# The order and the place of sixteen weight-band loads at the start of a fused spectral mixing and feed-forward kernel

## The chip, the cores and the metric

The kernel runs on one core of one Trainium2 chip. The metric is the device time of one execution in microseconds (us). Work is split over TensorE (PE; its weight loads are listed apart as PEld), VectorE (DVE), ScalarE (ACT), GpSimd (POOL) and SyncE (SP), whose queue issues every DMA of this kernel.

## The reference

For x of 8 batches x 3008 positions x 256 channels:

```python
X = np.fft.rfft(x, axis=1)
Yr = Xr @ w_r - Xi @ w_i + b_r
Yi = Xr @ w_i + Xi @ w_r + b_i
Y  = soft_threshold(Yr, 0.01) + 1j * soft_threshold(Yi, 0.01)
y  = np.fft.irfft(Y, n=3008, axis=1)            # 24064 tokens x 256
h  = y @ w_in                                   # 256 -> 2048
out = (h * np.clip(h + 3, 0, 6) / 6) @ w_out    # 2048 -> 256
```

All is float32, except that `w_in` and `w_out` arrive as float64.

## The kernel before

The 3008 positions are treated as 47 x 64. Stage 1 (`stage1`, seven sets for a batch, each loaded as a tile `xin`, or `x_hi`/`x_lo` for batch 0) does the transforms of length 47 and stores to a scratch tensor. `middle` (twelve pairs of frequency groups for a batch) loads a pair (`bt`, `f`), transforms over 64 (tile `X`), multiplies with the 256 x 256 weights (tiles `ps_a`, `tc`), applies the threshold, brings the parts into place (`zt`, by small DMAs, or for batch 0's last two pairs by VectorE copies on L482), transforms back (PE L498) and stores `pt` to a second scratch tensor. `segment` (seven for a batch) loads from there (`qt`, L531, two loads each) and does the inverse transform of length 47 into `raw` tiles of 512 tokens, on VectorE L562 and L574. `prepare` makes from a `raw` tile the seven operands `yb` of a Strassen-Winograd product. Then the feed-forward runs in units: 47 token chunks of 512 times 8 slices f of the hidden width. Unit (c, f) multiplies with `w_in` slice f (`phase_a` to `phase_d`, PE L165, sums on DVE L621), goes through the gate (ACT L680, DVE L682, ACT L136, DVE L137) and three units later is multiplied with `w_out` slice f (`down`, PE L711).

Every float32 operand is split in a high and a low half (`split`: high by an ACT copy, low by a DVE or POOL subtraction on L137), and a product is three matmuls.

The weights arrive as 16 bands of 512 KB in float64, eight of `w_in` and eight of `w_out`, band f of each for slice f; they are written below as in0 to in7 and out0 to out7. `decode` loads a band (`st`, L208) and turns the doubles into floats: per band two DVE operations on the words (L220, L221), three ACT operations, two DVE operations (L225, L229) and one on POOL (L230); an in-band then has four POOL subtractions (L247) and three splits, an out-band one split. `turn` moves each band in work one step on and, if told to, starts the next one from the list `bands`; its argument names the buffers that the band borrows: `EARLY` is `raw` for the load and three `yb`, `LATE` takes three sets of buffers by turns. The bands are started between the pairs of batch 0 and after that between the phases of the first units. A load of a band is put behind one chosen DMA on SP's queue (`tc.issue_after`).

The order on each engine's queue is made by a scheduler at build time from the program order, priorities, the buffers that are free and its own estimate of times; a queue then runs in that order. So loads may leave much earlier than the program text suggests, when their buffer is free, and an instruction that waits holds up all behind it on its queue.

In the kernel before the bands come in the order in0, in1, out0, in2, out1, in3, out2, in4, out3, in5, out4, in6, out5, in7, out6, out7. Two are started before batch 0's pairs, five between the pairs, three right after `prepare(0)`, the rest in the first units. Batch 1's stage 1 runs its first four sets among batch 0's pairs, the fifth `xin` is loaded after them with nothing that holds it back.

Of the kernel before, what the change touches and what calls it, by code (L numbers as in the profile page):

```python
# [101 lines left out]
def spectral_ffn(ctx: ExitStack, tc: tile.TileContext, x, w_r, w_i, bias, w_in, w_out, f47, f64, g64, sgn, out):  # L102
    nc = tc.nc
# [11 lines left out]
    def space(shape, dt, name, tag=None):  # L115
        tag = tag or name
        return sb.tile(shape, dt, name=name, tag=tag, bufs=depth.get(tag, 1))

    def twin(shape, dt, name, tag=None):

        t = space([P, 2, *shape[1:]], dt, name, tag)
        return t[:, 0], t[:, 1]

    def room(wide=False):
        if wide:
            return ps_b.tile([P, 512], F32, name="pb")
        return ps_a.tile([P, 512], F32, name="ps_a")

    def idle(q):

        pool, name = ((ps_o, "po0"), (ps_o, "po1"), (ps_c, "pd"), (ps_c, "pc"))[q % 4]
        return pool.tile([P, 512], F32, name=name)

    def split(hi, lo, src, on=None):

        nc.scalar.copy(out=hi, in_=src)  # L136
        (on or nc.vector).tensor_tensor(out=lo, in0=src, in1=hi.bitcast(F32), op=ALU.subtract)  # L137
# [38 lines left out]
    def run(g):  # L176
        for _ in g:
            pass

    nf = NFT // 2  # L180
# [22 lines left out]
    def decode(src, cut, tags):  # L203


        st = space([P, 2, 256, 2], I32, "st", tags[0])
        with tc.issue_after(stores[soon[made[0]]].ins if made[0] < len(soon) else pairs[1].ins):
            nc.sync.dma_start(out=st.rearrange("p a c w -> p a (c w)"), in_=cut(src, 2))  # L208
        yield
        high = st[:, :, :, 1]  # L210
        e = space([P, 2, 256], I32, "e", tags[1])
        m, r = (
            twin([P, 2, 256], I32, "m", tags[2])
            if len(tags) == 3
            else [space([P, 2, 256], I32, n, t) for n, t in zip("mr", tags[2:])]
        )
        mf, rf = m.bitcast(F32), r.bitcast(F32)
        v, s = nc.vector, nc.scalar

        v.tensor_scalar(out=e, in0=high, scalar1=20, scalar2=0x7FF, op0=ALU.arith_shift_right, op1=ALU.bitwise_and)  # L220
        v.tensor_scalar(out=m, in0=high, scalar1=0xFFFFF, scalar2=0xFFFFF, op0=ALU.bitwise_and, op1=ALU.bitwise_and)  # L221
        yield
        s.activation(out=rf, in_=e, func=AF.Relu, bias=top[:, :1], scale=-1.0)
        s.activation(out=e, in_=rf, func=AF.Relu, bias=top[:, 1:], scale=-(2.0**23))
        v.scalar_tensor_tensor(out=e, in0=high, scalar=-(1 << 31), in1=e, op0=ALU.bitwise_and, op1=ALU.bitwise_or)  # L225
        halves = st.rearrange("p a c w -> p (a c w)").bitcast(U16).rearrange("p (a c w) -> p a c w", a=2, w=4)
        s.activation(out=rf, in_=halves[:, :, :, 1], func=AF.Copy, bias=1.0, scale=2.0**-36)
        yield
        v.scalar_tensor_tensor(out=mf, in0=m, scalar=2.0**-20, in1=rf, op0=ALU.mult, op1=ALU.add)  # L229
        nc.gpsimd.tensor_tensor(out=mf, in0=mf, in1=e.bitcast(F32), op=ALU.mult)  # L230
        return mf, e.bitcast(F32)
# [22 lines left out]
    def out_band(f, tags):  # L254
        def cut(t, words):
            n = 512 * words
            return t[:, f * n : (f + 1) * n].rearrange("p (h c) -> p h c", h=2)

        w, _ = yield from decode(w_out, cut, tags)
        yield  # L260
        split(*(cut(t, 1) for t in wout_s), w)

    EARLY = (("raw", "yb", "yb", "yb"),)
    LATE = (("X", "bt", "tc"), ("z", "bt", "zt", "pt"), ("xin", "e", "xs"))
    bands = [(in_band, 0), (in_band, 1)]
    for f in range(nf):
        bands.append((out_band, f))
        if f + 2 < nf:
            bands.append((in_band, f + 2))
    bands = iter(bands)  # L270

    made, busy, ready, pairs, soon = [0], [], set(), [], (3, 8)

    def turn(how=None):

        for job in list(busy):
            if next(job[0], busy) is busy:
                busy.remove(job)
                ready.add(job[1])
        if how and made[0] < 2 * nf:  # L280
            make, f = next(bands)
            g = make(f, how[made[0] % len(how)])
            next(g)
            busy.append((g, (make, f)))
            made[0] += 1
# [6 lines left out]
    scr1, scr2, stores = {}, {}, []  # L292
# [7 lines left out]
    def stage1(b):  # L300
        scr1[b] = dram.tile([2, N1, NK, D], F32, name="scr1")
        sets = SEGS[-1:] + SEGS[:-1]
        xins = {}

        def load(i):
            n1, n = sets[i]
            rows, w = (R47, 2 * D) if n == 2 * J else (n * NK, D)
            if b == 0:
                xins[i] = spare[i]
            else:  # L310
                xins[i] = space([P, 2, 2 * D], F32, "xin", "raw" if b == 1 and i < 4 else "xin")
            at = n1 // J * 2 * D
            src = x[b, :rows, at : at + 2 * w].rearrange("p (s c) -> p s c", s=2)
            nc.sync.dma_start(out=xins[i][:rows, :, :w], in_=src)
            return rows, w

        shapes = [load(i) for i in range((len(sets), 2, 1)[min(b, 2)])]
        for i, (n1, n) in enumerate(sets):
            rows, w = shapes[i]
            xin = xins.pop(i)  # L320
            plus, minus = xin[:rows, 0, :w], xin[:rows, 1, :w]
            whole = b == 0 or b == 1 and i < 4
            e = space([P, 2 * D], F32, "e", "r" if whole else "e")[:rows, :w]
            on = nc.vector if whole else nc.gpsimd
            on.tensor_tensor(out=e, in0=plus, in1=minus, op=ALU.add)  # L325
            on.tensor_tensor(out=plus, in0=plus, in1=minus, op=ALU.subtract)
            for c, src in enumerate((e, plus)):
                q = 2 * i + c
                if whole:
                    ps = idle(q) if b else room(c == 1)  # L330
                    turns = f47_s[2][:rows, c * R47 : c * R47 + rows]
                    nc.tensor.matmul(out=ps[:rows, :w], lhsT=turns, rhs=src, start=True, stop=True)
                else:
                    xs = [t[:rows, :w] for t in twin([P, 2 * D], F32R, "xs")]
                    split(*xs, src, nc.gpsimd)
                    yield
                    ps = room()
                    product(ps[:rows, :w], [([t[:rows, c * R47 : c * R47 + rows] for t in f47_s[:2]], xs)], whole=True)
                home = ("a", "h", "z", "h", "xs", "h", "X")[q % 7] if b == 0 else "yb" if whole else "a"
                a = space([P, 2 * D], F32, "a", home)[:rows, :w]  # L340
                if home == "X":
                    space([P, 48], F32, "gap")
                nc.scalar.copy(out=a, in_=ps[:rows, :w])
                dst = scr1[b][c, n1 : n1 + n].rearrange("(g j) k d -> (j k) g d", g=w // D)
                stores.append(nc.sync.dma_start(out=dst, in_=a.rearrange("p (g d) -> p g d", d=D)))
                if c and i + 1 < len(sets) and i + 1 >= len(shapes) and not whole:
                    shapes.append(load(i + 1))
                yield
            if whole and len(shapes) < min(len(sets), 5 if i == 3 else i + 3 if i < 2 else 0):
                shapes.append(load(len(shapes)))  # L350

    bias_s = const.tile([P, 2 * D], F32, name="bias")
    sgn_s = const.tile([P, NK], F32, name="sgn")
# [33 lines left out]
    for n in range(2 * len(soon)):  # L387
        turn(EARLY if n < len(soon) else None)
    g64_s = g64_t[:2]
# [132 lines left out]
    def segment(b, k, tag="qt", aside=None):  # L522
        n1, n = SEGS[k]
        gr = 2 if n == 2 * J else 1
        rows = n // gr * NK
        w = n * NK
        t0 = b * S + n1 * N2
        qt = space([P, 2, 2, D], F32, "qt", tag)
        for cs in range(2):
            src = scr2[b][cs, n1 : n1 + n].rearrange("(g j) k d -> (j k) g d", g=gr)  # L530
            nc.sync.dma_start(out=qt[:rows, cs, :gr], in_=src)  # L531
        for c in range(t0 // T, (t0 + n * N2 - 1) // T + 1):
            if c not in raw:
                raw[c] = space([P, 2, T], F32, "raw")
# [11 lines left out]
        for dh in range(2):  # L546
# [3 lines left out]
                    out=ps[:, cs * w + g * rows : cs * w + (g + 1) * rows],  # L550
# [15 lines left out]
            for c, q, lo, hi in places(w, n * m):  # L566
                while lo < hi:
# [3 lines left out]
                    else:  # L571
# [3 lines left out]
                        out=raw[c][:, dh, q : q + size].rearrange("p (n q) -> p n q", n=r1 - row),  # L575
# [13 lines left out]
    yb = {}  # L589
# [157 lines left out]
    for i in range(3 * (NK // 2)):  # L747
        next(mid)
        if i % 3 == 0:
            turn(LATE[2:] if i == 27 else EARLY if i == 3 or i % 9 == 0 else None)  # L750
    run(mid)
    rest = stage1(1)
    for _ in range(8):
        next(rest)
# [146 lines left out]
```

## Time and profile before

| | us |
|---|---|
| median of 3 runs | 2559.48 (2558.84 to 2559.91) |
| profiled execution, its own time | 2560.95 |
| span of its trace | 2559.2 |
| PE busy in the span | 2502.8 (98%) |
| DVE busy | 1965.0 (77%) |
| ACT busy | 1825.9 (71%) |
| POOL busy | 756.2 (30%) |

Engines, lines and tiles are named as in the trace: "PE L498 pb<-zt" is a matmul on line 498 that reads `zt` and writes `pb`. A bracket at the end of a row tells how long the engine was idle ahead of it, and what it waited for. Names on the trace leave the band's number out: `st<-in_w_in` is the load of some band of `w_in`. SPq is SyncE's queue of DMA issues.

### The profile page before, as it was taken

What the parts mean: (1) busy time and instruction counts of PE and PEld (TensorE: products, weight loads), DVE (VectorE), ACT (ScalarE), POOL (GpSimd) and SP (SyncE); (2) the same over time, 40 slices, a digit from 0 to 9 for tenths busy, and PEclk for the clock granted to TensorE, in tenths of its full rate; (3) what the DMA queues carried; (4) which work ended last, traced back from release to release, by engine and by line L of the source; (5) the groups of instructions that cost most, each with busy time, mean ns of one, the idle gap of its engine ahead of it and who ended that gap; (6) DMA issues with size and microseconds to landing.
All of it is one profiled execution on the core that took longest, in us unless ns stands there. A gap on an engine that the chain in (4) does not pass through costs nothing.

```text
span 2559.2 us, 53456 instructions
## 1 busy us (share of the span) xinstructions
PE 2502.8 (98%) x20910; PEld 2447.6 (96%) x20910; DVE 1965.0 (77%) x3191; ACT 1825.9 (71%) x3587; POOL 756.2 (30%) x738
## 2 busy tenths in 40 slices
PE   6789999999999999999999999999999999999999
PEld 4579999999999999999999999999999999999999
DVE  7778878877787777777787777777777778677766
ACT  5467777777777777777777777777777777777776
POOL 3253342333223332323323333223321221121310
PEclk8889999999999999999999999999999999999999
DMA  7733432332222222333222222222222121110000
GB/s 244 224 88 103 126 103 83 91 91 68 60 84 78 86 72 67 85 86 89 60 75 84 72 79 84 71 78 80 74 78 59 53 66 51 37 41 17 12 18 17
DMA packets 150259, 200.54 MB, mean 78 GB/s; under 512 B 16863, under 2 KB 104215, under 8 KB 150007
## 3 DMA queue, kind: packets, MB, share of 16 engines
q1 hardware_dynamic: 150007, 197.13, 26.7%
q8 instruction: 164, 2.69, 0.5%
q14 instruction: 88, 0.72, 0.1%
HBM read 97.45 MB, written 74.97 MB: 67 GB/s over the span
## 4 chain that ended last, share of the span: by engine, by line
PE 90%; DMA 3%; DVE 3%; ACT 1%; POOL 1%; issue 1%; SPq 1%; ACTq 0%; POOLq 0%; DVEq 0%
PE po L711 38%; PE pb L165 19%; PE pc L165 10%; PE ps_a L145 7%; PE ps_a L165 7%; PE pd L165 5%; PE ps_a L142 3%; DMA xin<-in_x 1%; DMA zt<-tc 1%; DMA qt<-scr 0%; DMA x_lo<-in_x 0%; DVE r L682 0%; ACT r L680 0%; POOL e L325 0%; ACT gs L136 0%
## 5 line engine op out<-in xcount | busy, mean ns | idle before, releaser
L711 PE MATMUL po<-gs,w_out_hi 128*128 128x256 f32 x5984 | 1025.6, 277 | 0.0
L711 PEld LDWEIGHTS po<-gs,w_out_hi 128*128 128x128 f32 x5984 | 839.2, 188 | 1.6
L682 DVE SCALAR_TENSOR_TENSOR r<-r,h 128x1024 f32<-128x1024 f32 x375 | 476.4, 1270 | 269.4 <-ACT r L680 267.4
L711 PE MATMUL po<-gs,w_out_lo 128*128 128x256 f32 x2992 | 594.8, 278 | 0.9 <-ACT gs L136 0.5
L680 ACT ACTIVATE r<-h,three 128x1024 f32<-128x1024 f32 x375 | 433.0, 1155 | 191.5 <-DVE h L621 189.4
L165 PE MATMUL pb<-yb,w_in_hi 128*128 128x256 f32 x3008 | 568.2, 278 | 0.0
L137 DVE TENSOR_TENSOR gs<-r,gs 128x1024 fp32r<-128x1024 f32 x375 | 483.5, 1289 | 90.9 <-ACT gs L136 87.1
L136 ACT CAST gs<-r 128x1024 fp32r<-128x1024 f32 x375 | 394.3, 1051 | 109.3 <-DVE r L682 106.6
L165 PEld LDWEIGHTS pb<-yb,w_in_hi 128*128 128x128 f32 x3008 | 458.1, 189 | 3.1
L711 PEld LDWEIGHTS po<-gs,w_out_lo 128*128 128x128 f32 x2992 | 456.0, 188 | 3.8 <-ACT gs L136 2.2
L165 PE MATMUL pb<-yb,w_in_lo 128*128 128x256 f32 x1504 | 426.3, 286 | 2.0 <-ACT u L616 1.3
L137 POOL TENSOR_TENSOR yb<-T,yb 128x256 fp32r<-128x256 f32 x184 | 168.3, 917 | 841.9 <-ACT yb L136 828.2
L621 DVE TENSOR_TENSOR h<-pc,u 128x256 f32<-128x256 f32 x752 | 314.2, 418 | 113.1 <-PE pc L165 106.8
L616 ACT COPY u<-pb 128x256 f32<-128x256 f32 x752 | 279.5, 373 | 94.4 <-PE pb L165 80.5
L165 PE MATMUL pc<-yb,w_in_hi 128*128 128x256 f32 x1504 | 295.7, 278 | 0.0
L165 PEld LDWEIGHTS pb<-yb,w_in_lo 128*128 128x128 f32 x1504 | 283.5, 189 | 8.7 <-ACT u L616 2.8
L165 PEld LDWEIGHTS pc<-yb,w_in_hi 128*128 128x128 f32 x1504 | 228.9, 189 | 0.7
L165 PE MATMUL pc<-yb,w_in_lo 128*128 128x256 f32 x752 | 214.6, 285 | 4.7 <-DVE h L621 4.6
L616 ACT COPY p<-pb 128x256 f32<-128x256 f32 x376 | 140.1, 373 | 77.0 <-PE pb L165 75.1
L654 ACT COPY h<-pb 128x256 f32<-128x256 f32 x376 | 141.3, 376 | 49.4 <-PE pb L165 47.6
L621 DVE TENSOR_TENSOR h<-pd,p 128x256 f32<-128x256 f32 x376 | 156.6, 417 | 13.9 <-ACT p L616 11.8
L165 PEld LDWEIGHTS pc<-yb,w_in_lo 128*128 128x128 f32 x752 | 141.9, 189 | 9.4 <-DVE h L621 8.1
(165 smaller groups left out, 3939.4 us busy)
## 6 DMA issues: line engine op xcount, KB each, us to landing
bt<-scr SPq DMA_DIRECT2D x96, 256.0 KB, 3.0
scr<-pt SPq DMA_DIRECT2D x96, 256.0 KB, 2.4
zt<-tc SPq DMA_DIRECT2D x376, 64.0 KB, 2.0
out<-ot SPq DMA_DIRECT2D x93, 256.0 KB, 2.3
scr<-a SPq DMA_DIRECT2D x96, 240.0 KB, 2.7
qt<-scr SPq DMA_DIRECT2D x96, 240.0 KB, 3.5
xin<-in_x SPq DMA_DIRECT2D x42, 480.0 KB, 4.4
f<-in_f SPq DMA_DIRECT2D x96, 128.0 KB, 2.8
```

Of the source, the lines that this page charges most:

```text
L136: nc.scalar.copy(out=hi, in_=src)
L137: (on or nc.vector).tensor_tensor(out=lo, in0=src, in1=hi.bitcast(F32), op=ALU.subtract)
L142: first = first()
L145: m()
L165: last = nc.tensor.matmul(**m)
L616: nc.scalar.copy(out=t, in_=ps)
L621: nc.vector.tensor_tensor(out=to, in0=ps, in1=keep.pop((i, n)), op=ALU.add)
L654: marks["h", i] = nc.scalar.copy(out=hs[i][:, 1, :H], in_=pb)
L680: nc.scalar.activation(out=r, in_=h, func=AF.Relu, bias=three, scale=1.0)
L682: nc.vector.scalar_tensor_tensor(out=r, in0=r, scalar=6.0, in1=h, op0=ALU.min, op1=ALU.mult)
L711: last = nc.tensor.matmul(out=pos[dh][half], lhsT=w[:, ft * D + dh * P : ft * D + (dh + 1) * P], rhs=g[:, low, u, cols], start=opens and n ...
```

## The change

Four edits. The bands are sorted by `due`: in-band f at f, out-band f at f + 2.5, which gives in0, in1, in2, out0, in3, out1, in4, out2, in5, out3, in6, out4, in7, out5, out6, out7. Nine bands instead of seven are started by the end of batch 0's pairs: the two ahead of them, then steps 0, 3, 9 and 18 with `EARLY` buffers, 24 and 30 with `z` for the load and three `yb`, 27 with `xin`, `e` and `xs`; and `while busy: turn()` writes out what is left of them ahead of batch 1's first stage-1 sets and of the segments. A band started once the first two segments have been written is put behind the last of their four loads (`loads[3]`) instead of behind the second pair load. And the extra `xin` load of stage 1 (batch 1's fifth set) is put behind the last segment load written so far.

```diff
         st = space([P, 2, 256, 2], I32, "st", tags[0])
-        with tc.issue_after(stores[soon[made[0]]].ins if made[0] < len(soon) else pairs[1].ins):
+        if made[0] < len(soon):
+            ahead = stores[soon[made[0]]]
+        else:
+            ahead = loads[3] if loads else pairs[1]
+        with tc.issue_after(ahead.ins):
             nc.sync.dma_start(out=st.rearrange("p a c w -> p a (c w)"), in_=cut(src, 2))
...
+    def due(band):
+
+        make, f = band
+        return (f, 0) if make is in_band else (f + 2.5, 1)
+
     EARLY = (("raw", "yb", "yb", "yb"),)
     LATE = (("X", "bt", "tc"), ("z", "bt", "zt", "pt"), ("xin", "e", "xs"))
-    bands = [(in_band, 0), (in_band, 1)]
-    for f in range(nf):
-        bands.append((out_band, f))
-        if f + 2 < nf:
-            bands.append((in_band, f + 2))
-    bands = iter(bands)
-
+    SPARE = {i: ((("z", "yb", "yb", "yb"),), LATE[2:])[i // 3 % 2] for i in (24, 27, 30)}
+    bands = iter(sorted([(in_band, f) for f in range(nf)] + [(out_band, f) for f in range(nf)], key=due))
+
+    loads = []
...
             if whole and len(shapes) < min(len(sets), 5 if i == 3 else i + 3 if i < 2 else 0):
-                shapes.append(load(len(shapes)))
+                with tc.issue_after(loads[-1].ins) if loads else nullcontext():
+                    shapes.append(load(len(shapes)))
...
-            nc.sync.dma_start(out=qt[:rows, cs, :gr], in_=src)
+            loads.append(nc.sync.dma_start(out=qt[:rows, cs, :gr], in_=src))
...
         if i % 3 == 0:
-            turn(LATE[2:] if i == 27 else EARLY if i == 3 or i % 9 == 0 else None)
+            turn(SPARE[i] if i in SPARE else EARLY if i == 3 or i % 9 == 0 else None)
     run(mid)
+    while busy:
+        turn()
     rest = stage1(1)
```

## Rows read from the trace of the kernel before

**Rows 1.** The page: TensorE's busy tenths in 40 slices of 64 us.

```profile
PE   6789999999999999999999999999999999999999
```

**Rows 2.** Stages: busy of PE, PEld, DVE, ACT, POOL; clock, DMA share, GB/s.

```profile
64.00:76.00 12.00, 8.74 (x60) 7.14 (x58) 9.23 (x17) 5.12 (x12) 4.01 (x5) 0.94 0.84 234
112.00:126.00 14.00, 3.44 (x6) 0.83 (x4) 13.03 (x22) 9.85 (x20) 7.32 (x8) 0.63 0.84 260
134.00:165.00 31.00, 23.94 (x119) 20.26 (x118) 30.48 (x56) 22.68 (x50) 21.49 (x18) 0.72 0.29 82
165.00:204.00 39.00, 37.82 (x304) 36.10 (x305) 25.64 (x38) 28.19 (x56) 15.95 (x17) 1.00 0.29 78
```

**Rows 3.** TensorE's waits from 134 to 180 us: total, times, longest.

```profile
PE pc L165 <- DVE h L621: 4.6, 5, 1.7
PE pd L165 <- DVE h L621: 1.4, 1, 1.4
```

**Rows 4.** TensorE in order of time: start, duration, what, wait.

```profile
77.09 2.04 PE L498 MATMUL pb<-zt,g_all 128*128 128x512 f32 x2 [3.63 <-DMA zt<-tc]
...
112.38 1.02 PE L498 MATMUL pb<-zt,g_all 128*128 128x512 f32 x2
116.20 2.05 PE L498 MATMUL pb<-zt,g_all 128*128 128x512 f32 x2 [2.81 <-DVE zt L482]
126.09 0.78 PE L142 MATMUL ps_a<-f_all,qt 120*128 120x120 f32 x2 [7.84 <-DMA qt<-scr]
```

**Rows 5.** SyncE's queue in order of time: start, time to issue, what.

```profile
65.17 0.60 SPq L208 DMA_DIRECT2D st<-in_w_in  x1
...
118.90 0.32 SPq L501 DMA_DIRECT2D scr<-pt  x1
120.07 0.36 SPq L314 DMA_DIRECT2D xin<-in_x  x1
121.74 2.82 SPq L531 DMA_DIRECT2D qt<-scr  x4
124.66 0.38 SPq L208 DMA_DIRECT2D st<-in_w_out  x1
```

**Rows 6.** Landing us (last): load of 65.17, first qt, qt of 129.89.

```profile
st<-in_w_in SPq DMA_DIRECT2D x1, 512.0 KB, 9.3
...
qt<-scr SPq DMA_DIRECT2D x1, 240.0 KB, 4.3
...
qt<-scr SPq DMA_DIRECT2D x2, 240.0 KB, 3.2
```

**Rows 7.** VectorE in order of time, and one row of ScalarE.

```profile
111.99 0.42 DVE L221 TENSOR_SCALAR m<-st 128x512 int32<-128x512 int32 x1
...
115.47 0.59 DVE L482 COPY zt<-tc 64x256 f32<-64x256 f32 x2
...
129.47 0.36 ACT L560 COPY odd<-ps_a 128x240 f32<-128x240 f32 x1 [0.98 <-PE ps_a L145]
...
130.42 1.48 DVE L220 TENSOR_SCALAR e<-st 128x512 int32<-128x512 int32 x1 [1.58 <-DMA st<-in_w_out]
...
134.05 0.42 DVE L221 TENSOR_SCALAR m<-st 128x512 int32<-128x512 int32 x1
...
164.87 1.42 DVE L137 TENSOR_TENSOR w_out_lo<-m,w_out_hi 128x512 fp32r<-128x512 f32 x1
```

**Rows 8.** Decoding operations: ns min/median/max, first and last start in us.

```profile
L221 DVE TENSOR_SCALAR m<-st x7: 412/419/609, 112.0 to 152.1; 128x512 int32<-128x512 int32 x7
L225 DVE SCALAR_TENSOR_TENSOR e<-st,e x7: 676/942/1358, 116.1 to 156.6; 128x512 int32<-128x512 int32 x7
...
L137 DVE TENSOR_TENSOR w_in_lo<-m,w_in_hi x16: 285/540/1501, 28.2 to 154.0; 128x256 fp32r<-128x256 f32 x8, 128x128 fp32r<-128x128 f32 x8
L137 DVE TENSOR_TENSOR w_in_lo<-e,w_in_hi x8: 675/684/1771, 30.3 to 162.8; 128x512 fp32r<-128x512 f32 x8
...
L137 DVE TENSOR_TENSOR w_out_lo<-m,w_out_hi x8: 673/950/1750, 46.1 to 164.9; 128x512 fp32r<-128x512 f32 x8
```

## The prediction

> **What bounds the kernel now.** I read the page's tenths first. TensorE is at 90% or more in every slice but the first three [rows 1], so whatever this change does must show in the first 190 us or so: there TensorE stands still or runs slowly, and behind it a gain or loss only shifts the rest. Next the stages [rows 2]. From 112 to 126 TensorE is busy 3.4 of 14 us: this is the passage from batch 0's last pair to its first segment. From 134 to 165, the first units, it is busy 23.9 of 31 us at a mean granted clock of 0.72, so part of the time at the lower of its two levels, 1.2 instead of 2.4 GHz. From 165 it is busy 37.8 of 39 us at 1.00. In both troubled stretches VectorE is the full one: 13.0 of 14 and 30.5 of 31 us. From 165 to 204 it has 13.4 us free.
>
> Then the waits in order of time [rows 4]. The last pair's matmuls wait 2.81 us for a VectorE copy of `zt`; the first segment's wait 7.84 us for a `qt` load. Later, in the units, TensorE waits for the sums on VectorE, 6.0 us in six waits [rows 3]. There is one such place among the pairs too: 3.63 us at 77 us, for a `zt` transfer [rows 4].
>
> What VectorE does in that time is read from its own order [rows 7] and the decoding rows [rows 8]. L221 runs seven times from 112 us on: seven of the sixteen bands are decoded after 112, nine before. The bands' load order on SyncE's queue [rows 5] puts one `xin` load 1.7 us ahead of the four segment loads.
>
> **The change, part by part.** Nine bands also go with batch 0's pairs afterwards; seven stay, out3, in6, out4, in7, out5, out6, out7, and these may be loaded only behind the segment loads at about 122. So the edit moves no decoding out of the start as a whole. It clears it out of 112 to 126 and puts it behind. I go along the path.
>
> *Last pair.* Between 111.99 and the end of the last `zt` copy at 116.06 VectorE runs five word operations of bands, L220 and L221 [rows 7, 8]; one begins 0.33 to 0.45 us after the other, together 1.8 us. None can be there when no band's load is let through before the segments: -1.8. Bounds 0 (other work takes the places) and -2.8 (all of TensorE's wait [rows 4]).
>
> *Last matmuls.* Those at 112.38 took 1.02 us for two, those at 116.20, after 2.81 us of idling, 2.05: twice as long, the lower clock level [rows 4]. With a wait of 1.0 us instead of 2.8 I take the upper level: -1.0. Bounds 0 and -1.0.
>
> *Segment loads.* The first `qt` load, issued behind the `xin` load, took 4.3 us; two that were issued when little else moved took 3.2 [rows 5, 6]. The `xin` load now goes behind: -1.1. Bounds 0 and -2.0.
>
> *First segment's sums.* ScalarE's copy `odd` was done at 129.83, but VectorE's next instruction was L220 of a band whose load had been issued after the `qt` loads; it waited 1.58 us and took 1.48, so the segment's sums began 2.0 us late [rows 5, 7]. The same can come back, with another band in that place. I take it as gone: -2.0, with bounds -2.0 and +4.0. The upper one: three loads of 512 KB follow each other behind the segment loads, at 260 GB/s [rows 2] 2.0 us apart; now the first of such loads is waited for, and if it were the third, the sums would begin 4.0 us later still.
>
> *Pairs.* At 65.17 the tenth band's load is issued; it needed 9.3 us to land, in a stretch where the DMA engines are 84% busy [rows 2, 5, 6], and TensorE's wait of 3.63 us for `zt` ends it. A tenth band is now not loaded before the segments. Its 512 KB at 234 GB/s are 2.2 us of queue: -2.2. Against this, the nine hold six in-bands instead of five. By the undisturbed times an in-band costs VectorE 0.42 x 2 + 0.68 x 2 + 0.54 x 2 + 0.68 = 4.0 us, an out-band 0.42 x 2 + 0.68 x 2 + 0.67 = 2.9 [rows 8], with L220 and L229 taken as L221 and L225: +1.1. Together -1.1; bounds -3.6 (the whole wait) and +4.0 (one in-band's decoding stands fully in the pairs' way).
>
> The five gains make -7.0.
>
> *The seven bands in the first units.* Two in-bands and five out-bands cost 22.5 us by the undisturbed times. They will not be undisturbed: from 134.05 to 164.87 the trace holds 20 decoding instructions (the first and the last in [rows 7]), 17.8 us long where the undisturbed times give 11.7, a factor of 1.52. GpSimd is busy 21.5 of 31 us there [rows 2]. So 34 us against 17.8 there before: 16 us more. About 5 us of it fits between the first landing of a band and the first unit. Of the other 11, two thirds find room after 165, where VectorE has 13.4 us free [rows 2]: with three sets of buffers the seven go in three rounds, and only the first two need be over by then. Of the last third, 3.7 us, TensorE feels what it felt before: 6.0 us of waits for 17.8 us of decoding [rows 3, 7], 0.34 for each: +1.3. Bounds 0 (all hidden) and +5.4 (16 x 0.34). If the cover is gone, that is what it costs.
>
> The Trainium skill speaks against this part (SBUF — State Buffer, section "Who interferes with whom"): a VectorE instruction with two inputs in SBUF and a GpSimd instruction that reads SBUF share a read port, and whichever comes second stands still until the first is done. The trace agrees in kind: the same split on L137 took 673 to 1750 ns [rows 8]. By that rule the whole of GpSimd's 21.5 us could fall on the decoding, 44 us instead of 34, and the sum would be 1.1 us worse (10 / 3 x 0.34).
>
> The sorting itself costs nothing in issue: the same sixteen loads. No band is late by it: out3 and in6, loaded at about 124, are wanted by unit 6, and six units need 126 matmuls of `phase_a` to `phase_d` alone (seven products of three each), more than the 119 of all kinds that the stage to 165 holds [rows 2]. The extra `xin` load, now behind bands, feeds batch 1, whose next stage starts many units on; behind it on GpSimd stand its own sums.
>
> Sum: -7.0 + 1.3 = -5.7. The profiled execution took 2560.95, which gives 2555.3; it stands 1.5 above the median, so the median goes from 2559.48 to **2553.8**, 0.22% down. A change under 0.2%, 5.1 us, can hardly be told from none for this kernel.
>
> **Rivals.**
> *Gain kept whole* (0.09): the bands hide fully and the pairs gain all of their wait: -7.0 - 2.5 = -9.5, 2550. For it: VectorE's 13.4 us. Against: a queue in fixed order takes decoding when it is ready.
> *VectorE gives it back* (0.20): the 16 us fall where VectorE is full, +5.4: -1.6, 2557.9. For it: 30.5 of 31 us busy [rows 2]. Against: the seven are wanted later than that.
> *The way is not cleared* (0.09): the last pair and the segments wait for something else as long, the loads land as late, and only the pairs' -1.1 stays: 2558.4.
> *Bands ahead of the first gates* (0.18, slower): out3, in6 and out4 are written right after `prepare(0)`, ahead of unit 0, so they may stand on VectorE's queue before the first units' gates. Their 9.8 us times 1.52 are 14.9 us in which nothing reaches the second multiplication: -7.0 + 14.9 = +7.9, 2567. It decides from 12 us of decoding ahead of the first gate. For it: the program order, and that all three are loaded together. Against: bands stood in that place before too, and TensorE's longest wait for a sum was 1.7 us [rows 3].
>
> **How the numbers follow.** The forecast has 0.44, with a range of its own of 2550.5 to 2556.5; of this 0.37 lies beyond 5.1 us. Faster: 0.37 + 0.09 = 0.46. Same: 0.07 + 0.20 + 0.09 = 0.36. Slower: 0.18. The range runs from 2547.5, the whole gain and something of what the lower clock costs in 134 to 165, to 2565, short of the slower rival, whose upper part I leave out.
>
> **What the profile would show.** Right: nine bands' loads before 70 us and none until the four segment loads are issued at about 118; the first segment matmul at 121 to 122; its sums with no decoding row ahead that waits for a load; the unit stage from 130 with VectorE full until about 168 and TensorE waiting no more than 8 us for sums. The step at 77 us shows a wait under 2 us. Wrong: a wait of VectorE for a band's load ahead of L562 (then the sums come later than now); L221 rows of seven bands bunched before the first gate; or a pair stage that ends later than 116 us, which would undo all before the bands matter.

## The result, and the profile after

The changed kernel takes 2572.89 us (median of 6 runs, 2571.07 to 2578.03) against 2559.48 us (median of 6, 2556.21 to 2561.40): a ratio of 1.0051, 95% interval 1.0041 to 1.0061. It is 13.4 us slower, outside the stated range and on the other side of no change. The profiled execution took 2572.74 us with a span of 2571.0, 11.8 us more than the span before.

Up to the segments the path came out about as forecast. TensorE's last pair and the first segment matmul in the trace of the changed kernel (start, duration, what, wait), beside [rows 4]:

```profile
111.21 1.02 PE L505 MATMUL pb<-zt,g_all 128*128 128x512 f32 x2
113.55 1.10 PE L505 MATMUL pb<-zt,g_all 128*128 128x512 f32 x2 [1.32 <-DVE zt L489]
121.70 0.78 PE L142 MATMUL ps_a<-f_all,qt 120*128 120x120 f32 x2 [7.05 <-DMA qt<-scr]
```

The wait for `zt` is 1.32 instead of 2.81 us, the matmuls behind it take 1.10 instead of 2.05, and the first segment begins at 121.70 instead of 126.09, 4.4 us sooner. (Lines moved by the edit: L505 is the old L498, L212 the old L208, L224 and L225 the old L220 and L221, L229 and L233 the old L225 and L229.) SyncE's queue, and under it the landing times of the last `pt` store, the first `qt` load and the first held band, beside [rows 5, 6]:

```profile
118.93 1.80 SPq L538 DMA_DIRECT2D qt<-scr  x4
120.78 0.43 SPq L212 DMA_DIRECT2D st<-in_w_out  x1
...
scr<-pt SPq DMA_DIRECT2D x1, 256.0 KB, 3.5
...
qt<-scr SPq DMA_DIRECT2D x1, 240.0 KB, 2.7
...
st<-in_w_out SPq DMA_DIRECT2D x1, 512.0 KB, 5.5
```

The segment loads leave 2.8 us sooner and the first lands in 2.7 instead of 4.3 us. Now VectorE in order of time, beside [rows 7]:

```profile
112.21 1.19 DVE L489 COPY zt<-tc 64x256 f32<-64x256 f32 x4
126.34 0.43 DVE L224 TENSOR_SCALAR e<-st 128x512 int32<-128x512 int32 x1 [12.94 <-DMA st<-in_w_out]
...
127.02 0.40 DVE L569 TENSOR_TENSOR raw<-ps_a,odd 128x240 f32<-128x240 f32 x1
```

From the last `zt` copy to the landing of the first held band it does nothing for 12.94 us. The same stretch by engine (busy us and instructions of PE, PEld, DVE, ACT, POOL; clock, DMA share, GB/s), first the changed kernel, then the kernel before:

```profile
113.40:126.30 12.90, 5.70 (x23) 4.90 (x24) 0.00 (x1) 1.58 (x4) 0.00 (x0) 0.61 0.68 203
```

```profile
113.40:126.30 12.90, 2.26 (x3) 0.71 (x4) 11.93 (x19) 9.51 (x19) 7.62 (x8) 0.58 0.83 246
```

The 11.93 us of VectorE work of before did not vanish. The next stages of the changed kernel, beside [rows 2], and TensorE's waits from 134 to 180 us, beside [rows 3]:

```profile
112.00:126.00 14.00, 5.63 (x23) 4.60 (x23) 1.33 (x5) 2.77 (x6) 0.00 (x0) 0.65 0.67 196
134.00:165.00 31.00, 18.84 (x77) 15.88 (x77) 31.00 (x52) 21.91 (x48) 22.81 (x21) 0.61 0.28 84
165.00:204.00 39.00, 37.19 (x285) 35.22 (x284) 26.68 (x35) 27.74 (x55) 22.98 (x17) 0.97 0.22 58
```

```profile
PE pc L165 <- DVE h L628: 4.8, 3, 4.0
PE pd L165 <- DVE h L628: 3.2, 2, 2.0
PE pb L165 <- ACT yb L136: 1.7, 1, 1.7
PE pb L165 <- ACT h L661: 1.7, 1, 1.7
PE pb L165 <- DVE yb L137: 0.7, 2, 0.5
```

VectorE is busy for all of the 31 us, and TensorE gets through 77 matmul records there instead of 119, at a mean granted clock of 0.61 instead of 0.72. The five rows are all of TensorE's waits in that time, and none names a weight: it is not the late arrival of the bands that holds it up. There the 4.4 us of lead are lost, and more. After 204 us one more piece is lost. The stretch from 320 to 400 us, first after, then before:

```profile
320.00:400.00 80.00, 77.59 (x635) 74.92 (x634) 62.45 (x105) 58.06 (x122) 31.57 (x32) 1.00 0.39 111
```

```profile
320.00:400.00 80.00, 80.00 (x677) 78.80 (x677) 62.73 (x105) 57.66 (x120) 28.88 (x29) 1.00 0.35 101
```

TensorE is idle for 2.4 us there, although every band was decoded by 177 us.

How the 11.8 us between the two traces add up can be estimated from TensorE's records. Both traces hold the same 20910; each is counted here with the usual distance to the next one of its shape after 200 us (0.113 us for 128x256). Measured so, in us of TensorE's work, the changed kernel is 2 ahead at 126 us, 4 behind at 165, 6 at 205, 7 at 320 and 11 at 400, and stays there up to 600. About 8 us are lost from 126 to 205, and 4 from 320 to 400.

### The profile page after: what moved, and what is told of

It is laid out like the page before. It is cut to its first block, busy times and chain, and to the rows that moved or that the text cites. A ratio compares the mean times of both kernels' runs of the same rounds, so it can differ in the third digit from the quotient of the medians.

```text
span 2571.0 us, 53454 instructions
## 1 busy us (share of the span) xinstructions
PE 2504.6 (97%) x20910; PEld 2447.7 (95%) x20910; DVE 1964.5 (76%) x3191; ACT 1824.0 (71%) x3587; POOL 764.3 (30%) x738
## 4 chain that ended last, share of the span: by engine, by line
PE 88%; DVE 4%; DMA 3%; ACT 2%; POOL 1%; issue 1%; SPq 0%; ACTq 0%; POOLq 0%; DVEq 0%
PE po L718 38%; PE pb L165 19%; PE pc L165 9%; PE ps_a L145 7%; PE ps_a L165 6%; PE pd L165 5%; PE ps_a L142 3%; DMA scr<-a 1%; DMA zt<-tc 1%; DMA xin<-in_x 1%; POOL m L234 0%; DMA qt<-scr 0%; POOL e L331 0%; DVE r L689 0%; ACT r L687 0%
```

## The experiments

Three theories stood against each other. Theory 1: the hold behind the segment loads empties VectorE ahead of the segments, and its work falls on the first units. Theory 2: batch 1's fifth stage-1 set is late. Theory 3: the order by need, or nine bands among the pairs, costs it. The medians of the kernel before in the three groups of runs were 2559.23, 2558.94 and 2559.19 us.

**Undoing parts of the change.** First the hold on the bands:

```diff
-            ahead = loads[3] if loads else pairs[1]
+            ahead = pairs[1]
```

> The changed kernel with the bands' loads no longer held behind the segment loads; order, nine bands with batch 0's pairs and the held fifth stage-1 load stay. Theory 1 (VectorE lies idle for 13 us before the segments, because no band has landed, and decodes the seven bands in the first units instead): most of the 13.4 us comes back, 2559 to 2564, and VectorE's idle stretch before 126 us shrinks below 5 us. Theory 2 (the loss comes from batch 1's fifth stage-1 load, which lies behind the bands and waits for a buffer that a band holds): 2570 to 2574, little changed. Theory 3 (order by need or the nine bands among the pairs cost it): 2568 to 2574.

Measured: 2565.79 us, ratio 1.0030 (1.0019 to 1.0041). Half comes back, less than theory 1 said. VectorE does work ahead of the segments, 12.46 of 17 us, and from 108 us on is never idle for more than 2.42 us at a time, but the pairs end later. Its stage from 110 to 127 and its first segment matmul:

```profile
110.00:127.00 17.00, 10.53 (x53) 6.71 (x51) 12.46 (x25) 8.50 (x15) 3.04 (x3) 0.84 0.74 221
...
132.95 0.78 PE L142 MATMUL ps_a<-f_all,qt 120*128 120x120 f32 x2 [8.37 <-DMA qt<-scr]
```

The segments begin at 132.95, 11.2 us later than in the changed kernel, and the kernel is 7 us faster all the same. When the segments begin is not what decides.

Then the hold on the fifth stage-1 load:

```diff
-                with tc.issue_after(loads[-1].ins) if loads else nullcontext():
-                    shapes.append(load(len(shapes)))
+                shapes.append(load(len(shapes)))
```

> The changed kernel with the fifth stage-1 load of batch 1 no longer held; all else as changed. Theory 1: 2570 to 2574, since the bands are as late as before. Theory 2: most of it comes back, 2560 to 2565, the fifth set's load is issued before 122 us instead of 153.7 and TensorE's loss between 320 and 400 us is gone. Theory 3: 2570 to 2574.

Measured: 2570.90 us, ratio 1.0049 (1.0034 to 1.0064). As an effect of this hold theory 2 falls: the load, free to go, left no sooner, at 153.04 us against 153.71:

```profile
153.04 0.36 SPq L320 DMA_DIRECT2D xin<-in_x  x1
```

Both holds undone (both edits above):

> The changed kernel with neither the bands nor the fifth stage-1 load held; what is left of the change is the order by need and nine bands with the pairs. Theory 1 and theory 2 together: 2556 to 2562, equal to the kernel before or a little faster. Theory 3: 2568 to 2574.

Measured: 2562.27 us, ratio 1.0014 (1.0005 to 1.0023), 0.3 us above the range of theories 1 and 2. The order by need and the nine bands together cost some 3 us. The order alone put back, both holds kept:

```diff
-    bands = iter(sorted([(in_band, f) for f in range(nf)] + [(out_band, f) for f in range(nf)], key=due))
+    bands = [(in_band, 0), (in_band, 1)]
+    for f in range(nf):
+        bands.append((out_band, f))
+        if f + 2 < nf:
+            bands.append((in_band, f + 2))
+    bands = iter(bands)
```

> The changed kernel with the bands in the order of the kernel before; both loads held and nine bands with the pairs as changed. Theory 1 and 2: 2569 to 2577, as slow as the changed kernel. Theory 3, if it is the order: 2559 to 2564.

Measured: 2568.31 us, ratio 1.0032 (1.0019 to 1.0044). The order takes a part, but with the old order the hold still costs 9 us; the value lies just under the range of theories 1 and 2.

**One part alone, put on the kernel before.** The hold on the bands (the same `ahead = loads[3] if loads else pairs[1]`, with the segment loads noted in `loads`):

> The kernel before with one part of the change: bands started once the segments are written are loaded behind the fourth segment load. Seven are through with the pairs as before, so nine are now late. Theory 1 predicts a loss larger than that of the changed kernel's hold, since two bands more wait: 2566 to 2576. Theory 3 (order or nine): 2557 to 2562.

Measured: 2573.00 us, ratio 1.0058 (1.0041 to 1.0075). This one part gives the whole loss, with nine bands late instead of seven. Its trace holds the clearest contrast: the first segment matmul, VectorE's first operation of the segments with the idle time ahead of it, and two stages:

```profile
117.47 0.78 PE L142 MATMUL ps_a<-f_all,qt 120*128 120x120 f32 x2 [7.79 <-DMA qt<-scr]
...
121.25 0.41 DVE L567 TENSOR_TENSOR raw<-ps_a,odd 128x240 f32<-128x240 f32 x1 [12.81 <-ACT odd L565]
...
140.00:165.00 25.00, 17.24 (x110) 15.41 (x110) 25.00 (x47) 20.37 (x40) 12.32 (x12) 0.82 0.21 64
165.00:205.00 40.00, 31.76 (x221) 29.77 (x219) 32.83 (x38) 27.20 (x53) 27.33 (x21) 0.87 0.16 40
```

The segments begin 8.6 us sooner than before, after 12.81 us in which VectorE is idle; then it is full to 165, and TensorE is busy 31.8 of 40 us after that.

The order alone, and the nine bands alone (the `SPARE` line, the `turn` that uses it and `while busy: turn()`):

> The kernel before with the bands in order of need and nothing else. If the order has a price of its own (the changed kernel with the old order was 4.6 us faster than the changed kernel): 2562 to 2566. If it is only the hold that costs: 2556 to 2562.

> The kernel before with nine bands started by the end of batch 0's pairs instead of seven, what is left of them written out ahead of the segments, and nothing else: old order, nothing held. If the nine slow the pairs: the first segment matmul comes later than 128 us and the time is 2562 to 2568. If not: 2555 to 2561.

Measured: 2562.55 us, 1.0013 (1.0004 to 1.0023), and 2564.03 us, 1.0017 (1.0006 to 1.0028); the runs of the second range from 2555.5 to 2566.8. With the nine, VectorE is busy 84.8 instead of 78.6 us up to 110, and the first segment matmul comes at 132.64; but that trace is of the fastest of its ten runs (2555.5), so it does not show where the median loses. So theory 3 holds for some 3 to 5 us with either part alone; the two don't add up (both together, without holds, 3.0 us). Why the order costs anything was not found.

**The price of the work itself.** The seven late bands loaded and split, but not decoded:

```diff
+        late = made[0] >= 9
         yield
         high = st[:, :, :, 1]
         e = space([P, 2, 256], I32, "e", tags[1])
+        if late:
+            return high.bitcast(F32), e.bitcast(F32)
```

> The changed kernel with the seven late bands loaded and split as before, but not decoded: their two word operations and two combining operations on VectorE, three on ScalarE and the product on GpSimd are left out, so the weights of these bands are other numbers. If VectorE's decoding in the first units is the price (theory 1): 28 VectorE operations fewer, 15 us undisturbed and 23 us as they ran, at least 8 us of the 13.4 come back, 2553 to 2565, and VectorE is no longer full from 127 to 165. If it is the buffers that the bands hold, or the order: 2569 to 2574, since loads and buffers are held about as long.

Measured: 2554.39 us, ratio 0.9981 (0.9972 to 0.9990), 18.5 us less than the changed kernel, with the same load order and its first segment matmul at 122.01. The four kinds of decoding operation took VectorE 19.8 us in the changed kernel (28 rows from 126.34 to 171.3 us added up); here they are gone, with seven operations each of three kinds on ScalarE and one on GpSimd. The stage that was full:

```profile
134.00:165.00 31.00, 26.78 (x181) 24.73 (x180) 22.42 (x41) 21.03 (x46) 15.21 (x16) 0.86 0.35 99
```

181 matmul records instead of 77, the clock at 0.86 instead of 0.61. The mechanism of theory 1 is shown: with the same loads in the same order and the segments as early, the loss is gone once the decoding is. But the 18.5 us are not the price of VectorE's 19.8 us alone. ScalarE and GpSimd are relieved too, the splits of the late bands take 7.4 instead of 9.9 us, and the buffers come free sooner: the fifth stage-1 load leaves at 140.94, and from 320 to 400 TensorE is busy 79.90 of 80 us. By the count of TensorE's work about 14 us are gained by 205 us and 3 from there to 400.

**Where the late bands stand.** The three that rank ahead of the first unit in the program order moved behind it:

```diff
-    for n in range(3):
-        turn(LATE)
-        turn()
...
-        turn(LATE if q % 2 == 0 else None)
+        turn(LATE if q % 2 == 0 and q >= 4 else None)
```

> The changed kernel with the three bands that are written right after the first prepare moved behind the first unit, so that all seven late bands come after the first unit's own operations in the program order. If the bands' rank ahead of the first operands and gates is what VectorE's full stretch costs: 2558 to 2566. If VectorE's idle 13 us ahead of the segments is lost whatever the rank: 2569 to 2575.

Measured: 2571.97 us, ratio 1.0056 (1.0039 to 1.0073): no change. VectorE stays full from 140 to 165 us. Rank is not the matter. The buffers: late bands take only the first two of the three sets (`LATE[:2]` in the three calls after batch 0's pairs):

> The changed kernel with the late bands taking only the first two sets of buffers by turns, never the stage-1 buffers xin, e, xs. If bands in these buffers hold back batch 1's fifth stage-1 set (its load at 153.7 us also when it was no longer put behind the segments) and through it batch 1's segments, that load leaves before 130 us and TensorE loses less than 1 us between 320 and 400 us instead of 2.4: 2567 to 2571. If the buffers do not matter: 2571 to 2578, since seven bands in two sets take longer.

Measured: 2572.66 us, ratio 1.0053 (1.0034 to 1.0072). The fifth set's load and the stretch from 320 to 400 us:

```profile
128.26 0.43 SPq L320 DMA_DIRECT2D xin<-in_x  x1
...
320.00:400.00 80.00, 79.77 (x666) 78.13 (x665) 64.74 (x103) 60.55 (x124) 30.32 (x31) 1.00 0.38 109
```

The load leaves at 128.26, and TensorE loses 0.2 us there instead of 2.4. So that loss goes with the bands in the stage-1 buffers: in the changed kernel one that holds `xin` until 153 us keeps batch 1's remaining sets waiting, and the first pair load of batch 1 leaves at 208.95 instead of 188.21. But with two sets the decoding ends later (188 instead of 176 us) and costs more before 205 us (TensorE busy 31.4 of 40 us from 165, instead of 38.2), so the total is the same.

**The hold at another place.** The late bands behind the last pair's load instead of the fourth segment load:

```diff
-            ahead = loads[3] if loads else pairs[1]
+            ahead = pairs[11] if loads else pairs[1]
```

> The changed kernel with the late bands held behind the last pair's load instead of the fourth segment load, some 20 us sooner, so that they can land and be decoded in the 13 us in which VectorE stands idle ahead of the segments. Theory 1: 2557 to 2564, and VectorE busy for more than 11 of the 17 us from 110 to 127. If decoding there only delays the last pair and the segments by as much: 2566 to 2573.

Measured: 2562.99 us, ratio 1.0014 (1.0004 to 1.0023): 9.9 us less than the changed kernel. Three stages of it:

```profile
110.00:127.00 17.00, 2.77 (x5) 1.23 (x6) 16.43 (x27) 14.07 (x25) 7.74 (x8) 0.59 0.90 272
...
140.00:165.00 25.00, 19.52 (x107) 16.87 (x107) 20.45 (x34) 14.21 (x33) 13.96 (x13) 0.72 0.23 60
165.00:205.00 40.00, 39.27 (x327) 38.37 (x328) 27.71 (x41) 28.56 (x57) 17.28 (x18) 1.00 0.30 78
```

VectorE works 16.4 of 17 us ahead of the segments, these begin at 126.27, later than in the changed kernel by 4.6 us, and TensorE is at full pace from 165 on. From 320 to 400 it is idle for 1.4 us here too, though the fifth stage-1 load left at 130.99 and batch 1's first pair load at 186.63; so that stretch is not explained by this load alone. The same with the old order:

> As the run before, with the bands in the order of the kernel before. If the hold is all that costs, equal to it within 3 us; if the order has a price of its own, some 4 us faster: 2553 to 2560.

Measured: 2564.11 us, ratio 1.0022 (1.0011 to 1.0034), within 3 us of the last one; here the order by need shows no price. No run with all its work in it was faster than the kernel before.

## Why the prediction was wrong, point by point

*Last pair* (-1.8), *last matmuls* (-1.0) and *segment loads* (-1.1): right in kind and nearly in size; *pairs* (-1.1): right in size. Wait 2.81 to 1.32 (-1.5), matmuls 2.05 to 1.10 (-0.95), landing 4.3 to 2.7 (-1.6), the matmuls at 112.38 now at 111.21 (-1.2). The `pt` store gave back 0.7 (2.8 to 3.5). Together 4.4 at the first segment matmul; 5.0 were forecast.

That the pairs fit is luck. The wait of 3.63 us at 77 us is gone as forecast, but VectorE, busy with the bands, now holds TensorE up four times between 63 and 86 us, 5.3 us in all; two of the waits:

```profile
63.77 0.39 PE L165 MATMUL ps_a<-w_r_hi,X 128*128 128x256 f32 x1 [1.57 <-DVE tc L466]
70.57 0.67 PE L338 MATMUL po<-xin,f_all 96*96 96x256 f32 x2 [1.50 <-DVE xin L332]
```

TensorE is idle longer from 76 to 112 us (2.7 instead of 1.3 us); its granted clock was 1.00 there instead of 0.92, a term that the sum did not have.

*First segment's sums* (-2.0): this wait came back, as the prediction had allowed, though for the first of the held loads and not the third. `odd` was done at 125.44, but VectorE's next instruction was L224 of the first held band, which landed at 126.3; the sums began at 127.02. They had begun at 131.8 [rows 7], so 4.8 us of lead are left where 7.0 were forecast, and the step is worth -0.4.

*The seven bands in the first units* (+1.3, bounds 0 to +5.4): the step that failed. The whole work was nearly right: decoding and splits of the late bands took 29.7 us from 126 on (28 and 9 rows of VectorE), forecast 34. The extra work was not: the 16 us come from setting all of the seven bands' decoding against the part of the old one that ran from 134 on. From 134 on it was 24.0 us against 17.8, 6.2 more where 11 were forecast.

The price was far too low. I took 0.34 us for each us, from TensorE's waits that name VectorE [rows 3], and +5.4 as the most that it could cost. By the count of TensorE's work some 8 us were lost from 126 to 205. In a stretch where VectorE is full, work put in can move everything behind it by its whole length; the named waits hold only a part of that, the rest stands in the lower clock and in waits with other names (`yb`, `h` from ScalarE). I had set no more than 8 us of waits for sums as a sign of being right: there were 4.8 + 3.2 = 8.0, and the time was wrong all the same.

The undecoded run puts the price at 18.5 for 19.8, 0.93, as an upper value; the 14 us gained by 205 us make it 0.7, still twice what I took. Why 6.2 us of extra decoding cost 8 is not told apart: in the same stretch TensorE's clock is lower, and the segments' sums and the first units' own work wait with the decoding for the same engine.

*The cover*: VectorE's 13.4 free us after 165 [rows 2] were to take two thirds of it. Its busy time from 165 to 204 rose by 1.0 us only, from 25.6 to 26.7. The first three bands were loaded together at 121 us, the last at 143.7, and all but 2.7 of the 29.7 us of their work had begun by 165, wanted or not.

I had even written that the edit "moves no decoding out of the start as a whole" and clears VectorE from 112 to 126. The simple account was at hand: 11.9 us of VectorE in 113.4 to 126.3, ahead of the stretch that VectorE bounds, go to nothing. That 11.9 or 12.94 lies so near the 13.4 is partly luck: VectorE made up some of it elsewhere (3.0 us more busy up to 76, 1.6 from 126 to 134), and a third of the loss stands between 320 and 400.

*No cost for the extra `xin` load*: its hold was indeed harmless, but bands that hold the stage-1 buffers delayed the set by 34 us (120.07 to 153.71), and between 320 and 400 TensorE was idle for 2.4 us and fell back by about 4 us of work. I priced neither.

*Rivals*: the slower one, bands ahead of the first gates, has the nearest time (2567) and the wrong mechanism: the first gate came 2.0 us later (ScalarE's gate operation at 154.49 instead of 152.47), not 15, and rank did nothing. Its mark, 12 us of decoding ahead of the first gate, was met from 126 us on (19.7 us), but so it had been before (16.0). "VectorE gives it back" has the right mechanism, at about half the price or less.

The two-input rule of the Trainium skill (SBUF — State Buffer, section "Who interferes with whom") agrees again in kind: in the changed kernel L229 ran from 678 to 1747 ns. But since the undecoded run took operations from VectorE, ScalarE and GpSimd at once, their shares in the 18.5 us are not told apart.

What stays open: the 3 to 5 us that order and nine bands cost by themselves, near what these runs can tell; and why TensorE falls back between 320 and 400, where only the buffers were tried.

## What to carry to other kernels

Before a load is moved behind another, ask which engine consumes it and what that engine does in the time thus emptied: idle time ahead of a stretch in which this engine is full cannot be made up in it. Starting the critical path 4 or 9 us sooner was worth nothing here, because the engine that bounds the next stage entered it with more work. And a price taken from named waits was too low by a factor of two or more: in a full stretch count the work itself, before and after over the same stretch.

## What the runs showed of the hardware that I had not expected

A VectorE instruction with one input is held up beside GpSimd as well. In the changed kernel L225 took 421 ns in the median and 1494 once, while a GpSimd product ran; VectorE and then GpSimd, in order of time:

```profile
130.50 1.49 DVE L225 TENSOR_SCALAR m<-st 128x512 int32<-128x512 int32 x1
...
130.29 1.42 POOL L234 TENSOR_TENSOR m<-m,e 128x512 f32<-128x512 f32 x1 [49.50 <-DMA qt<-scr]
```

It began 0.2 us after the product, at 130.50, and ended 0.3 us after the product's end, at 131.99. It is no single case: in the fourteen traces here 116 of these one-input instructions (the two word operations of decoding) took more than 0.45 us, and every one ended 0.28 to 0.29 us after the end of a GpSimd instruction that had begun before it. Twenty others began beside a GpSimd instruction and were not slowed. The Trainium skill (SBUF — State Buffer, section "Who interferes with whom") has a place for it: some VectorE operations with a single source, among them this kind, can use a mode that takes the shared port pair, and then whoever comes second stands still. The ends, always the same time after the other's end, agree with standing still until then, and not with a slower pace; whether the instructions ran in that mode no run shows.
